# Second attention of a fused attention and MoE kernel: the exps' key blocks added by VectorE before the row sums

## The chip, the cores and the metric

The kernel runs on one core of one Trainium2 chip. The metric is the device time of one execution in microseconds (us), the median of three runs; lower is better.

## The reference

Attention with a soft cap, for q, k, v of shape (4 batches, 12 heads, 448, 64), is followed by two dense layers (each with a nonlinear part between two matrix products):

```python
scores = scale * np.matmul(q, k.transpose(0, 1, 3, 2))
scores = cap * np.tanh(scores / cap)
scores = scores - np.max(scores, axis=-1, keepdims=True)
attn = np.exp(scores)
attn = attn / (np.sum(attn, axis=-1, keepdims=True) + 1e-09)
return np.matmul(attn, v).astype(np.float32)
...
x = np.ascontiguousarray(attn_out.transpose(0, 2, 1, 3)).reshape(B * S, H * D)
x = _moe_ref(x=x, **moe_kwargs)
return _moe2_ref(x=x, **moe2_kwargs)
```

The sums of the exps over the keys (`np.sum(attn, ...)`) are what this case is about.

## The kernel before

The work is done in two halves of two batches each (`hb` 0 and 1, from line 657). A half is `attention`, then `moe1`, then `moe2`. The last block of the first half's `moe2` is woven into the start of the second half's attention (`rest`).

`attention` (line 229) goes over 12 pairs of heads, p = 0 to 11 (n = 12). The 448 keys of a head are three blocks of 128 and one of 64; the scores are kept with the keys on the partitions and the 448 queries on the columns. A pair has seven score tiles of 128x448: for each of the three full blocks one tile for each head (b = 2r + hh), and one tile x that holds the 64-key blocks of both heads (64 partitions for each). They lie in `t[:, 0..6]`, with `t[:, 6]` from x.

The functions of a pair, in the order of the data:
- `load`, `load_v`, `fetch`: DMAs from POOL's queue (q and k, v, and weights for the next stage). `kq` and `vf` have three buffers.
- `split_qk` (252): VectorE writes the high and low part of q and k (`kqh`, `kql`), two operations of 960 columns.
- `scores` (265): TensorE, 18 matmuls into six PSUM banks (`s`), then three for x into a bank of tag `o`.
- `tanh` (286), `exp` (296): ScalarE, x first and then the two halves of `s`; one exp over all seven tiles, in place in `t`.
- `values` (301): TensorE, 16 fp32 matmuls on four 32-column tiles; the trace records two matmuls for each fp32 matmul.
- `sums` (309): TensorE with columns of ones as weights. For each of the two heads the three full blocks and the shared one are summed: eight matmuls on four 32-column tiles in two accumulating rounds, so that partitions 0 and 64 hold the two partial sums of head 0 and 32 and 96 those of head 1. For the last pair the tiles have 64 columns, and all four blocks of a head accumulate into its 64 partitions (lines 312 to 318).
- `evict_v` (326): VectorE copies the values out of PSUM. `evict_s` (332): ScalarE copies the sums out of PSUM (97 partitions), and SP issues two DMAs that spread them over 56 partitions (`rs`).
- `finish1` (339): VectorE adds the two partial sums and takes the reciprocal; SP writes them to DRAM (`rd`). `finish2` (346): SP reads them back over all partitions (`rb`). `finish3` (357): VectorE multiplies the values, and writes the high and low part (`xh`, `xl`) for the next stage, three operations. The last pair takes `finish_last`.

The order of every engine's work inside `attention` is that of the program text (`manual_schedule`, line 660). The loop at line 383 runs i from -5 to 11; in one iteration each function works for another pair:

```python
at(i, values)
at(i + 1, tanh)
at(i, sums)
at(i - 2, finish1)
at(i - 3, finish2)
at(i - 5, finish3)
at(i + 3, split_qk)
at(i, evict_v)
at(i + 2, scores)
at(i + 1, exp)
...
at(i, evict_s, m=n - 1)
```

`at` leaves out pairs below 0 or from 12 on, so that `finish3` starts with i = 5 and `split_qk` ends with i = 8. PSUM has eight banks: six for `s` and two for tag `o`, which values, sums and x take in turn: x of pair i + 2 comes into the bank of the values of pair i, the values of pair i + 1 into that of the sums of pair i, and the sums of pair i + 1 into that of x of pair i + 2. After the loop come the `finish` functions that are left (lines 406 to 414). `moe1` (422) is not ordered by hand: its first matmuls (`first`, line 438; recorded at lines 434 and 436) are woven by the program's scheduler into the last iterations. They go over batch 0 of the half with three column blocks, then over batch 1 in steps, the pairs finished last at the end.

Of the kernel before, what the change touches and what calls it, by code (L numbers as in the profile page):

```python
# [9 lines left out]
F32 = mybir.dt.float32  # L10
# [4 lines left out]
ALU = mybir.AluOpType  # L15
# [14 lines left out]
def fused_kernel(ctx, tc, qk_in, v, cap, w1, w2, w3, w4, gln, out):  # L30
    nc = tc.nc
    B, H, S, D = 4, 12, 448, 64
    DM = H * D
    P = 128
    CP = 56
    Q = 32
# [22 lines left out]
    psum = {}  # L59
# [30 lines left out]
    ones = const.tile([P, 3, D], F32, name="ones")  # L90
# [50 lines left out]
    def early():  # L141

        units = [(f"1_{c}_{half}_{i}", w1u[(c * 2 + half) * (NK // 2) + i])
                 for c in range(2) for half in range(2) for i in range(NK // 2)]
        units += [(f"2_0_{d}", w2u[d]) for d in range(NK)]
        units = units[:WA]
        stage = {}

        def fetch(k):
            key, src = units[k]  # L150
            if key in saved:
                w = wp.tile([P, 2, 512], F32R, tag="w", name="w")
                nc.gpsimd.dma_start(w.bitcast(F32), saved[key].bitcast(F32))
                ahead[key] = w
            else:
                stage[k] = words(src, nc.sync if k == 0 else nc.gpsimd)

        def high(k):
            key = units[k][0]
            if k in stage:  # L160
                w = wp.tile([P, 2, 512], F32R, tag="w", name="w")
                ahead[key] = w
                stage["f", k] = narrowed(stage.pop(k))

        def mid(k):
            if ("f", k) in stage:
                nc.scalar.copy(ahead[units[k][0]][:, 0], stage["f", k])

        def low(k):
            if ("f", k) in stage:  # L170
                key = units[k][0]
                w = ahead[key]
                nc.vector.tensor_tensor(w[:, 1], stage.pop(("f", k)), w[:, 0].bitcast(F32), ALU.subtract)
                pending.append((key, w))

        return fetch, high, mid, low
# [52 lines left out]
    def attention(ap, hb, xh, xl, rest=None):  # L229
        pairs = [(bb, j) for bb in range(HB) for j in range(NP)]  # L230
        n = len(pairs)
        raw, qk, vs, sc, ts, os_, so, fin, rss, rds, rbs = ({} for _ in range(11))
        fetch, high, mid, low = early()

        def load(p):
# [73 lines left out]
        def sums(p):  # L309
# [9 lines left out]
            for rr in range(2):  # L319
                for g in range(4):  # L320
# [2 lines left out]
                    w = ones[:, 0, :Q] if r < 3 else ones[:, 1 + hh, :Q]  # L323
                    nc.tensor.matmul(o[cs, :S], w, t[:, 6 if r == 3 else 2 * r + hh], start=(rr == 0), stop=(rr == 1))  # L324

        def evict_v(p):
            if p < n - 1:
                ou = ap.tile([P, S], F32, tag="ou", name="ou", bufs=7)
                nc.vector.tensor_copy(ou, os_.pop(p)[:, :S])
                fin[p] = ou  # L330

        def evict_s(p):
            su = ap.tile([P, S], F32, tag="su", name="su", bufs=2)
            nc.scalar.copy(su[:3 * Q + 1], so.pop(p)[:3 * Q + 1, :S])
            rs = rss[p] = ap.tile([CP, 2, 2 * S // CP], F32, tag="rs", name="rs", bufs=4)
            for k in range(2):
                nc.sync.dma_start(rs[:, k], su[2 * Q * k:2 * Q * k + Q + 1:Q])
# [39 lines left out]
        def at(p, fn, *a, m=n):  # L377
            if 0 <= p < m:
                fn(p, *a)
# [3 lines left out]
        for i in range(-5, n):  # L383
            e = i + 2
            at(i, values)
            at(i + 1, tanh)
            at(i, sums)
            at(i - 2, finish1)
            at(i - 3, finish2)
            at(i - 5, finish3)  # L390
            at(i + 3, split_qk)
            at(i, evict_v)
            at(i + 2, scores)
            at(i + 1, exp)
            if hb == 0 and i == 0:
                nc.scalar.activation(gcol, guard, AF.Exp)
            if rest and i == -1:
                rest[2]()
            at(i, evict_s, m=n - 1)
            at(e - 2, mid, m=WA)  # L400
            at(i + 5, load)
            at(e, fetch, m=WA)
            at(i + 3, load_v)
            at(e - 3, low, m=WA)
            at(e - 1, high, m=WA)
# [251 lines left out]
    for hb in range(2):  # L657
        xh, xl = xtiles()
        with pools(f"a{hb}", ("t",), ("kqh", "kql"), ("ou",), ("rb", "rs", "su"), None) as ap, banks(f"pa{hb}", ("s", 2), ("o", 2)):
            with tc.manual_schedule(engines=ORD):  # L660
                attention(ap, hb, xh, xl, rest)
        yh, yl = xtiles()
        if hb == 0:
            nc.sync.dma_start(glt, gln.rearrange("(c p) -> p c", p=P))
        with pools(f"m{hb}", ("gh", "gl"), ("wx",), ("acc",), None) as mp, banks(f"pm{hb}", ("a", 2), ("b", 2)):
            moe1(mp, xh, xl, yh, yl)
        with pools(f"n{hb}", ("h2g",), ("wx",), ("lh0", "ll0"), None, ("e",), ("lh1", "ll1")) as mp, banks(f"pn{hb}", ("a", 2), ("b", 2)):
            rest = moe2(mp, hb, yh, yl)
# [63 lines left out]
```

## Time and profile before

| | |
|---|---|
| median of three runs | 913.27 us (913.23 to 913.3) |
| profiled execution | 918.84 us |
| its span | 917.1 us |
| mean granted clock of TensorE | 0.999 |
| TensorE busy | 911.1 us (99%) |
| VectorE busy | 584.3 us (64%) |
| ScalarE busy | 420.8 us (46%) |
| POOL busy | 46.7 us (5%) |

The span runs from the first to the last instruction of the profiled execution. Times in rows are us from the start of the span. PE is TensorE, ACT is ScalarE, DVE is VectorE. The second attention goes from about 452 to 554 us.

### The profile page before, as it was taken

Reading aid. Unit: us, or ns where it says so; the run is one execution under the profiler, and the core shown is the slowest. Engines: PE = TensorE matmul, PEld = TensorE weight load, DVE = VectorE, ACT = ScalarE, POOL = GpSimd, SP = SyncE. Lnnn points to the kernel's source line nnn. Section 1 sums busy time; section 2 is a strip of 40 time slices with the busy share of each in tenths; the row PEclk is TensorE's granted clock in tenths of the full one; section 3 lists DMA queues with packets and bytes.
Section 4 is the critical chain, followed back from the end, with each engine's and each line's share of the span. In section 5 each row is a group of like instructions: output and inputs, shape, how many; then the busy total and the mean of one; then the engine's idle time right before and its main releaser. Section 6 shows DMA issues by size and latency. Waiting matters only on the chain.

```text
span 917.1 us, 13131 instructions
## 1 busy us (share of the span) xinstructions
PE 911.1 (99%) x5258; PEld 732.8 (80%) x5258; DVE 584.3 (64%) x919; ACT 420.8 (46%) x480; POOL 46.7 (5%) x88
## 2 busy tenths in 40 slices
PE   8999999999999999999999999999999999999998
PEld 5444699999999988888854448999999999888887
DVE  6687989999999990987334535881452634306751
ACT  6999276555263322343278880862421502113311
POOL 2211000000000000001122100000000000000000
PEclk9999999999999999999999999999999999999999
DMA  8554680795875972730255532333232332231301
GB/s 286 182 179 149 235 309 24 240 366 175 294 256 194 304 242 101 245 132 36 108 208 193 176 90 89 126 120 111 92 115 92 126 105 93 69 115 42 130 36 51
DMA packets 46424, 142.98 MB, mean 156 GB/s; under 512 B 10460, under 2 KB 13532, under 8 KB 46364
## 3 DMA queue, kind: packets, MB, share of 16 engines
q1 hardware_dynamic: 39180, 112.95, 36.3%
q0 software_dynamic: 7040, 29.20, 9.2%
q8 instruction: 41, 0.67, 0.3%
q14 instruction: 19, 0.16, 0.1%
q10 hardware_dynamic: 144, 0.00, 0.0%
HBM read 98.64 MB, written 43.33 MB: 155 GB/s over the span
## 4 chain that ended last, share of the span: by engine, by line
PE 98%; DMA 1%; ACT 0%; DVE 0%; issue 0%
PE hp L434 17%; PE op L490 17%; PE hp L436 9%; PE op L492 9%; PE o L307 8%; PE s L275 5%; PE hp L227 4%; PE hp L225 4%; PE hp L226 4%; PE so L324 4%; PE oab L594 2%; PE oab L590 2%; PE oab L591 2%; PE x L281 2%; PE tp L539 1%; PE oab L592 1%
## 5 line engine op out<-in xcount | busy, mean ns | idle before, releaser
L434 PE MATMUL hp<-xl,w 128*128 128x448 f32 x384 | 116.3, 369 | 0.0
L434 PE MATMUL hp<-xh,w 128*128 128x448 f32 x384 | 116.2, 369 | 0.0
L436 PE MATMUL hp<-xh,w 128*128 128x448 f32 x384 | 115.9, 368 | 0.0
L492 PE MATMUL op<-gh,w 128*128 128x448 f32 x336 | 96.8, 368 | 0.0
L490 PE MATMUL op<-gh,w 128*128 128x448 f32 x336 | 96.6, 368 | 0.0
L490 PE MATMUL op<-gl,w 128*128 128x448 f32 x336 | 96.6, 368 | 0.0
L434 PEld LDWEIGHTS hp<-xh,w 128*128 128x128 f32 x384 | 72.1, 188 | 8.8 <-issue 1.5
L434 PEld LDWEIGHTS hp<-xl,w 128*128 128x128 f32 x384 | 72.1, 188 | 8.6 <-issue 1.4
L307 PE MATMUL o<-t,vf 128*32 128x448 f32 x768 | 77.8, 542 | 0.1
L436 PEld LDWEIGHTS hp<-xh,w 128*128 128x128 f32 x384 | 72.1, 188 | 7.2
L299 ACT ACTIVATE t<-t,shift,capt 128x3136 f32<-128x3136 f32 (+2 forms) x26 | 72.7, 2806 | 0.7
L499 DVE TENSOR_TENSOR acc<-op,acc 128x448 f32<-128x448 f32 x72 | 42.1, 622 | 46.9 <-PE op L492 46.7
L490 PEld LDWEIGHTS op<-gh,w 128*128 128x128 f32 x336 | 63.1, 188 | 6.4
L490 PEld LDWEIGHTS op<-gl,w 128*128 128x128 f32 x336 | 63.1, 188 | 6.4
L492 PEld LDWEIGHTS op<-gh,w 128*128 128x128 f32 x336 | 63.1, 188 | 6.3
L292 ACT ACTIVATE t<-s,tscale 128x1344 f32<-128x1344 f32 x48 | 63.5, 1378 | 6.3 <-PE s L275 6.3
L225 PE MATMUL hp<-w,xh 128*128 128x512 f32 x168 | 65.5, 390 | 0.0
L227 PE MATMUL hp<-w,xl 128*128 128x512 f32 x168 | 65.4, 389 | 0.0
L226 PE MATMUL hp<-w,xh 128*128 128x512 f32 x168 | 65.4, 389 | 0.0
L462 ACT ACTIVATE u<-hp 128x896 f32<-128x896 f32 x32 | 29.4, 920 | 75.8 <-PE hp L436 75.8
L468 DVE SCALAR_TENSOR_TENSOR gf<-u,hp 128x896 f32<-128x896 f32 x32 | 34.9, 1089 | 45.5 <-ACT t L464 45.5
L476 ACT CAST gh<-gf 128x896 fp32r<-128x896 f32 x32 | 30.2, 945 | 72.7 <-PE op L492 49.2
(150 smaller groups left out, 1645.8 us busy)
## 6 DMA issues: line engine op xcount, KB each, us to landing
d<-w SPq DMA_DIRECT2D x69, 512.0 KB
w<-d SPq DMA_DIRECT2D x56, 512.0 KB
st<-in_moe_w_out_dram SPq DMA_DIRECT2D x35, 512.0 KB
st<-in_moe_w_in_dram SPq DMA_DIRECT2D x25, 512.0 KB
kq<-in_qk_dram POOLq DMA_DIRECT2D x21, 480.0 KB, 4.2
w<-d POOLq DMA_DIRECT2D x13, 512.0 KB, 5.1
st<-in_moe_w_in_dram POOLq DMA_DIRECT2D x11, 512.0 KB, 5.2
vf<-in_v_dram POOLq DMA_DIRECT2D x22, 256.0 KB, 2.9
```

What stands on the lines that cost most here:

```text
L225: nc.tensor.matmul(ps, sh, mh, start=first, stop=False)
L226: nc.tensor.matmul(ps, sh, ml, start=False, stop=False)
L227: nc.tensor.matmul(ps, sl_, mh, start=False, stop=last)
L275: nc.tensor.matmul(s[b // 3][:, b % 3, :S], st[rows, cs], mv[rows, KW:], start=first, stop=last)
L292: nc.scalar.activation(t[:, 3 * half:3 * half + 3], s[half][:, :, :S], AF.Tanh, scale=tscale)
L299: nc.scalar.activation(t[:, sl], t[:, sl], AF.Exp, bias=shift, scale=capt)
L307: nc.tensor.matmul(o[cs, :S], vf[:, r, cs], t[:, 6 if r == 3 else 2 * r + g // 2], start=(r == 0), stop=(r == 3))
L434: nc.tensor.matmul(hp[:, g, :S], wh[:, ms], xs[g][i], start=(kk == 0 and i == 0), stop=False)
L436: nc.tensor.matmul(hp[:, g, :S], wl[:, ms], xs[g][0], start=False, stop=(kk == NK - 1))
L490: nc.tensor.matmul(op[:, g, :S], wh, gg[i][:, g], start=(m == 0 and i == 0), stop=False)
L492: nc.tensor.matmul(op[:, g, :S], wl, gg[0][:, g], start=False, stop=(m == nm - 1))
L499: nc.vector.tensor_tensor(a, op[:, g, :S], a, ALU.add)
```

## The change

It concerns the second attention alone (`hb` 1). A new function `presum` lets VectorE add the three full key blocks of each head, `t[:, 0:2]`, `t[:, 2:4]` and `t[:, 4:6]`, into a tile `m` of 128x896 (two adds, the second in place). `sums_added` takes the place of `sums`: the ones multiply `m` and the shared block, four matmuls in one round of four 32-column tiles for a pair, and for the last pair four matmuls on 64-column tiles. `presum` of pair i + 1 stands after its exp in the loop. `evict_s` copies by VectorE instead of ScalarE, and stands directly after `evict_v` instead of after the exp.

```diff
+        def presum(p):
+            t = ts[p]
+            m = sm[p] = ap.tile([P, 2, S], F32, tag="sm", name="sm", bufs=2)
+            nc.vector.tensor_tensor(m, t[:, 0:2], t[:, 2:4], ALU.add)
+            nc.vector.tensor_tensor(m, m, t[:, 4:6], ALU.add)
+
+        def sums_added(p):
+            t, m = ts.pop(p), sm.pop(p)
+            o = so[p] = psum["o"].tile([P, 512], F32, tag="o", name="so")
+            if p == n - 1:
+                for hh in range(2):
+                    nc.tensor.matmul(o[D * hh:D * (hh + 1), :S], ones[:, 0], m[:, hh], start=True, stop=False)
+                for hh in range(2):
+                    nc.tensor.matmul(o[D * hh:D * (hh + 1), :S], ones[:, 1 + hh], t[:, 6], start=False, stop=True)
+                return
+            for g in range(4):
+                hh = g % 2
+                w, b = (ones[:, 0, :Q], m[:, hh]) if g < 2 else (ones[:, 1 + hh, :Q], t[:, 6])
+                nc.tensor.matmul(o[Q * g:Q * (g + 1), :S], w, b, start=True, stop=True)
+
...
-            nc.scalar.copy(su[:3 * Q + 1], so.pop(p)[:3 * Q + 1, :S])
+            (nc.vector.tensor_copy if hb else nc.scalar.copy)(su[:3 * Q + 1], so.pop(p)[:3 * Q + 1, :S])
...
-            at(i, sums)
+            at(i, sums_added if hb else sums)
...
             at(i, evict_v)
+            if hb:
+                at(i, evict_s, m=n - 1)
             at(i + 2, scores)
             at(i + 1, exp)
+            if hb:
+                at(i + 1, presum)
...
-            at(i, evict_s, m=n - 1)
+            if not hb:
+                at(i, evict_s, m=n - 1)
```

## Rows read from the trace of the kernel before

**Rows 1.** The page: busy time by engine; the chain's shares by engine.
```profile
PE 911.1 (99%) x5258; PEld 732.8 (80%) x5258; DVE 584.3 (64%) x919; ACT 420.8 (46%) x480; POOL 46.7 (5%) x88
...
PE 98%; DMA 1%; ACT 0%; DVE 0%; issue 0%
```

**Rows 2.** The chain that ended last, one loop iteration: start, us, engine, tile, line.
```profile
474.29 3.15 PE o L307 x32
477.44 1.50 PE so L324 x16
478.94 2.02 PE s L275 x18
480.96 0.82 PE x L281 x3
481.78 3.14 PE o L307 x32
```

**Rows 3.** ScalarE's timeline, one iteration and the last exp: start, us [idle before, releaser].
```profile
504.28 0.64 ACT L290 ACTIVATE t<-x,tscale 128x448 f32<-128x448 f32 x1 [0.86 <-PE x L281]
...
507.49 3.01 ACT L299 ACTIVATE t<-t,shift,capt 128x3136 f32<-128x3136 f32 x1
510.40 0.51 ACT L334 COPY su<-so 97x448 f32<-97x448 f32 x1
...
544.92 3.01 ACT L299 ACTIVATE t<-t,shift,capt 128x3136 f32<-128x3136 f32 x1
```

**Rows 4.** VectorE's timeline over the same iteration.
```profile
504.28 0.66 DVE L257 CAST kqh<-kq 128x960 fp32r<-128x960 f32 x1 [1.71 <-PE x L281]
504.97 1.16 DVE L258 TENSOR_TENSOR kql<-kq,kqh 128x960 fp32r<-128x960 f32 x1
507.45 0.62 DVE L329 COPY ou<-o 128x448 f32<-128x448 f32 x1 [1.32 <-PE o L307]
508.00 0.22 DVE L341 SCALAR_TENSOR_TENSOR rs<-rs,gcol 56x16 f32<-56x16 f32 x1
508.25 0.24 DVE L342 RECIPROCAL rs<-rs 56x16 f32<-56x16 f32 x1
508.42 0.55 DVE L366 TENSOR_TENSOR ou<-ou,rb 128x448 f32<-128x448 f32 x1
509.00 0.39 DVE L367 CAST xh<-ou 128x448 fp32r<-128x448 f32 x1
509.43 0.63 DVE L368 TENSOR_TENSOR xl<-ou,xh 128x448 fp32r<-128x448 f32 x1
```

**Rows 5.** The chain at the loop's end: seven hp matmuls, last values, last sums.
```profile
546.32 0.60 PE hp L434 x2
...
547.74 0.20 PE hp L434
547.98 3.21 PE o L307 x32
551.19 3.16 PE so L317 x16
```

**Rows 6.** VectorE on 896 columns: timeline in the MoE stage; groups of the whole run.
```profile
577.17 1.09 DVE L472 SCALAR_TENSOR_TENSOR gf<-w,gf 128x896 f32<-128x896 f32 x1
578.18 1.08 DVE L471 TENSOR_TENSOR t<-hp,t 128x896 f32<-128x896 f32 x1
579.30 1.23 DVE L473 COPY_PREDICATED gf<-mk,t 128x896 f32<-128x896 uint8 x1
...
L477 DVE TENSOR_TENSOR gl<-gf,gh 128x896 fp32r<-128x896 f32 x32 | 34.8, 1091 | 26.8 <-ACT gh L476 25.9
```

**Rows 7.** Wait instructions before the values, whole run: ns min/median/max.
```profile
L307 PEldq EVENT_SEMAPHORE  x24: 51/51/1277, 11.2 to 544.3; - x24
```

**Rows 8.** After the loop: VectorE's last finish3; ScalarE's first activation of the next stage.
```profile
563.01 0.63 DVE L368 TENSOR_TENSOR xl<-ou,xh 128x448 fp32r<-128x448 f32 x1
...
574.21 0.92 ACT L462 ACTIVATE u<-hp 128x896 f32<-128x896 f32 x1 [25.87 <-PE hp L436]
```

More of the change, by code (lines that the diff above doesn't have):

```diff
@@ L231, in attention @@
         n = len(pairs)
-        raw, qk, vs, sc, ts, os_, so, fin, rss, rds, rbs = ({} for _ in range(11))
+        raw, qk, vs, sc, ts, os_, so, fin, rss, rds, rbs, sm = ({} for _ in range(12))
         fetch, high, mid, low = early()
```

## The prediction

> **What bounds the kernel now.** I read the page first, then the chain that ended last over the second attention, then the timelines of ScalarE and VectorE for one iteration of its loop, last the end of the loop. The page says that TensorE is busy for 99% of the span and holds 98% of the chain [rows 1], so time comes off only where TensorE gets less to do, or is lost where it starts to wait. The chain through one iteration is TensorE without a hole: values 3.15 us, sums 1.50, the next scores 2.02, their shared block x 0.82 [rows 2], together 7.49 us, and the next values begin 7.49 us later. The reader should see that no other engine is in it.
>
> ScalarE starts a pair's tanh when its x is done (504.28) and ends the exp at 510.50, that is 6.22 us later; then comes the copy of the sums (0.51 us), and 0.86 us were waited for x [rows 3]. VectorE works in two pieces and waited 1.71 us before the first [rows 4]. Neither is far from TensorE's period: that is what decides this case.
>
> At the end of the loop the exp of pair 11 runs to 544.92 + 3.01 = 547.93 [rows 3], and values(11) begin at 547.98 [rows 5]: they wait for ScalarE, with 0.05 us from the recorded end to the start. The gap before them, from 546.32, is filled by seven matmuls of the next stage [rows 5].
>
> **Sums on TensorE.** A pair's sums are 8 fp32 matmuls on 32-column tiles, recorded as 16, in 1.50 us [rows 2]: four steps of four tiles, 0.375 each. The change leaves 4 matmuls, recorded as 8, two such steps: 0.75 us. Eleven pairs give 11 x 0.75 = 8.25 us. The last pair works on 64-column tiles, 16 records in 3.16 us [rows 5]; 8 stay, so 1.58 us goes. Gross 9.83 us, and TensorE's iteration becomes 6.74 us. No gain beyond this is to be had, since nothing else leaves TensorE. The same number of switches between tile shapes stays, so I price them at nothing.
>
> **ScalarE** loses 11 copies of 0.51 us. It gains nothing in time: tanh starts with x. But its 6.22 + 0.05 us from x to the values must now fit in 6.74, which leaves 0.47. It fits.
>
> **VectorE** gains the copy of the sums and two adds of 128x896 for each pair. What counts is the distance from start to start. From the timeline [rows 4]: split 0.69 + 1.08, copy of the values 0.55, the two small steps of finish1 0.25 + 0.17, the three of finish3 0.58 + 0.43 + 0.55, together 4.30 us. Where an idle time follows, I took the recorded time less 0.08, as in the MoE stage, where an operation of 1.09 us is followed after 1.01 by one that doesn't need it and one of 1.08 after 1.12 by one that does [rows 6]. The copy of the sums has the width of the copy of the values and also reads PSUM: 0.55. The adds have no row of their own. The nearest is the subtraction with two fp32 operands in SBUF over the same 896 columns, 1.091 us [rows 6]; the second add needs the first, so 1.12 + 1.01 = 2.13 for the pair. From below: the in-place product over 448 columns took 0.55, and from 448 to 960 columns a subtraction grew from 0.63 to 1.16, 1.04 ns per column [rows 4], so an add is 1.01 and the pair about 1.96. From above: the copy with a mask over 896 columns, 1.23 [rows 6], so about 2.40. I take 2.13, since that row has the same operand places and size.
>
> VectorE's iteration is then 4.30 + 0.55 + 2.13 = 6.98 us against TensorE's 6.74. But this full load occurs in few iterations: finish3(i-5) exists from i = 5, split_qk(i+3) up to i = 8. Outside i = 5 to 8 VectorE has at most 5.4 us and the cover is there. In these four the copy of the values comes late for x(i+2), which takes over its PSUM bank (two banks hold values, sums, x in turn), and TensorE waits 0.24 us each: 0.96 us. With the bounds of the adds it is 0.3 to 2.0 us.
>
> Rows show that VectorE's next operation starts 0.08 us before the recorded end of the one before it, where it doesn't need its result [rows 6]. The Trainium skill ("VectorE: DVE Perf Modes", The DRAIN you can't avoid) speaks against this: the next operation does not start until the pipe is empty, though it allows that one which is not held starts earlier. By that rule in its strict form the load would be the sum of the recorded durations, 7.27 us, the wait 4 x 0.53 = 2.1 us and the time 905.6 us. The trace has the overlap, so the sum above stays.
>
> **The waits that are moved.** The adds stand in VectorE's queue behind both copies and wait for the exp; queued behind them are finish1, finish3, the split and the next copy of the values. The exp ends 6.27 us after its x, which with a period of 6.74 is 0.47 before the next values start; the adds end 1.66 after it, and the sums need them at 3.15. So TensorE does not wait for the adds. The copy of the sums now frees a bank from VectorE instead of ScalarE: the next values wait for it, but in a full iteration it ends 0.55 after the copy of the values, while x alone takes 0.82. The sums' two DMAs on SP keep their place among SP's other DMAs and are issued earlier. POOL's loads wait as before on the values and on the split, iterations ahead of their use. Values wait now on two engines (exp, copy of the sums); should each cost one more wait instruction, 51 ns [rows 7], that is 0 to 0.6 us. I take 0: the values have such a wait now, one for each pair, and the chain goes from x to values without a hole (480.96 + 0.82 = 481.78).
>
> **The end.** sums(10) become 0.75 us shorter, but values(11) follow exp(11), whose start is tied to x(11). The gap grows by 0.75 us. The seven matmuls fit the old gap within 0.05 us, so I take it that the order, made outside the hand-written part, follows the gap's length and puts three or four more there; else 0.75 us is lost. VectorE's tail begins one pair of adds later. It ended at 563.64, while the first activation of the next stage waited until 574.21 [rows 8]. Ahead of that lie 12 matmuls at 0.20 us [rows 5] which need the pair that VectorE finishes last, so they start some 8 us after the tail; 2.1 us of adds and 1.6 us from TensorE coming earlier fit under that.
>
> **Sum.** 8.25 + 1.58 - 0.96 = 8.87 us. The profiled execution took 918.84 us (span 917.1), 5.57 more than the median 913.27; the stage worked on is the same, so I take the difference off the median: 904.4 us.
>
> **Rivals.**
> *VectorE binds harder.* For it: 0.24 us of excess rests on overlaps of hundredths, and each late x also delays tanh, exp and the next adds. A full circle (x 0.82, tanh and exp 6.27, adds 2.13, finish 1.98, split 1.77, copy 0.62 and 0.05 of signal) is 13.6 us for two periods, 6.82 each, so little has to be added to it. Against: five of the eleven iterations have no finish3 and two no split. If these four keep the old 7.49, the loss is 3.0 us; with waits of 0.6 for values and the end's 0.75 the gain is 5.5, 907.8 us; with adds at their upper bound alone it is 7.8, 905.5 us. The Trainium skill ("TensorEngine Tiling (Array Packing)", PSUM Bottleneck) says that after tiling the copy out of PSUM may become the bottleneck and that both ScalarE and VectorE are to be used for it; here both copies go to VectorE. Of itself that is the 0.55 us counted above: the trace bears it out only in so far as VectorE's load passes TensorE's.
>
> *The gap at the end is not filled.* 905.1 us. Against it stands the good fit of the seven.
>
> *Slower: the adds cost double.* Two fp32 streams out of SBUF beside ScalarE's long in-place exp could go at half rate. Pair 4.26: a full iteration 9.11, so 2.37 x 4; in the others the circle without finish3 is (9.99 + 4.26) / 2 = 7.13, 0.39 over, x 6. Loss 11.8 against 9.83: 915.3 us. It decides from about 1.9 us for an add; the 1.091 of [rows 6], a mean over 32, is against it.
>
> *Hardly a gain.* The step of four tiles costs 0.375 us in a stream of four; if two in a row keep a fixed part, or adds lie between 1.5 and 1.9 us, the change does not bring what its count says: about 912.
>
> **How the numbers follow.** Forecast 0.50, own range 903.4 to 905.4; gap unfilled 0.17; VectorE harder 0.25; hardly a gain 0.04; slower 0.04. The gross gain of 9.83 sets the lower end, 903.3 with a tenth for the spread of the runs; VectorE's case sets the upper, 907.8; outside are the last two cases and a tail. Within 0.2%, about what a measurement of this kernel can tell, is 911.4 to 915.1. So faster 0.92, same 0.04, slower 0.04.
>
> **What would show it.** Sums in the chain at 0.75 us for 8 records and 1.58 for the last; a period of 6.74 up to i = 4, near 7.0 in i = 5 to 8, then 6.74; in these four a wait of x on the copy of the values, and nowhere on the adds; adds of 1.0 to 1.1 us; ten or eleven matmuls before values(11). Wrong would be: adds over 1.2 us, values waiting on the exp or the copy of the sums in every iteration, a period over 7.0 in the light ones, or the next stage waiting for VectorE's tail.

## The result and the profile after

| | before | after |
|---|---|---|
| median, us (runs) | 913.28 (6; 911.55 to 915.42) | 904.91 (6; 903.03 to 908.23) |
| ratio, 95% interval | | 0.9904 (0.9886 to 0.9923) |
| profiled execution, us (span) | 918.84 (917.1) | 907.26 (905.5) |
| first scores of the second attention | 452.51 | 450.31 |
| ScalarE's first activation behind it | 574.21 | 563.13 |
| the stage between them | 121.70 | 112.82 |

The median fell by 8.37 us, where 8.87 was forecast. The two profiled executions differ by 11.58, and only 8.88 of that lies in the stage that was changed: the second attention began 2.20 us earlier, and 0.50 came behind the stage. A total spreads over some microseconds from run to run; the stage moved by 0.2 to 0.3 (a second trace of the changed kernel, below, has 112.51, one of the kernel before 121.47). The stage is therefore the measure in what follows, taken in every trace from the same two instructions.

The page of the changed kernel, busy time by engine and the chain's shares, against [rows 1]:

```profile
PE 897.6 (99%) x5162; PEld 727.9 (80%) x5162; DVE 613.4 (68%) x954; ACT 416.7 (46%) x469; POOL 48.1 (5%) x88
...
PE 84%; DVE 10%; DMA 3%; issue 1%; ACT 1%; SPq 0%; DVEq 0%
```

TensorE lost 13.5 us of busy time and VectorE gained 29.1; the matmul records fell by 96, that is 11 x 8 + 8. VectorE's 10% of the chain are only in small part this change: 18 us of them lie in the second attention, some 73 in the first half, which is the same in both kernels. The chain's shares differ between executions of one kernel: the second trace of the kernel before (last experiment) has TensorE at 88% and VectorE at 8%, where [rows 1] has 98% and 0%.

The chain of the changed kernel through one early iteration, against [rows 2]:

```profile
471.36 3.15 PE o L307 x32
474.51 0.75 PE so L344 x8
475.26 2.05 PE s L275 x18
477.31 0.81 PE x L281 x3
478.12 3.14 PE o L307 x32
```

The sums take 0.75 us where they took 1.50, and the next values begin after 6.76 us instead of 7.49. Nothing but TensorE is in it. One of the full iterations looks different. The timeline of VectorE, changed kernel, against [rows 4] (L349 copies the values, L354 the sums, L329 and L330 are the adds):

```profile
503.80 0.62 DVE L349 COPY ou<-o 128x448 f32<-128x448 f32 x1
504.33 0.61 DVE L354 COPY su<-so 97x448 f32<-97x448 f32 x1
504.86 1.08 DVE L329 TENSOR_TENSOR sm<-t 128x896 f32<-128x896 f32 x1
505.98 1.09 DVE L330 TENSOR_TENSOR sm<-sm,t 128x896 f32<-128x896 f32 x1
506.99 0.22 DVE L361 SCALAR_TENSOR_TENSOR rs<-rs,gcol 56x16 f32<-56x16 f32 x1
507.24 0.24 DVE L362 RECIPROCAL rs<-rs 56x16 f32<-56x16 f32 x1
507.41 0.55 DVE L386 TENSOR_TENSOR ou<-ou,rb 128x448 f32<-128x448 f32 x1
508.00 0.39 DVE L387 CAST xh<-ou 128x448 fp32r<-128x448 f32 x1
508.43 0.63 DVE L388 TENSOR_TENSOR xl<-ou,xh 128x448 fp32r<-128x448 f32 x1
508.97 0.66 DVE L257 CAST kqh<-kq 128x960 fp32r<-128x960 f32 x1
509.66 1.16 DVE L258 TENSOR_TENSOR kql<-kq,kqh 128x960 fp32r<-128x960 f32 x1
510.73 0.62 DVE L349 COPY ou<-o 128x448 f32<-128x448 f32 x1
```

No idle time is noted on any of these lines: VectorE runs without a hole, and its round, from copy to copy, is 6.93 us. That is longer than TensorE's 6.74 to 6.76, so TensorE waits. The round before it, the first that holds both finish3 and the split, still had a hole:

```profile
497.91 1.09 DVE L329 TENSOR_TENSOR sm<-t 128x896 f32<-128x896 f32 x1 [1.35 <-ACT t L299]
```

There VectorE waited 1.35 us for the exp, and from then on had no idle time until the copy at 503.80. In this first iteration it is the path from the exp over the adds, finish and split to the copy that is late for x, in the next three VectorE's load. The view of the waits over the second attention, changed kernel (who waited, for whom: us in total, times, longest; PEld is TensorE loading the weights of a matmul, and `issue` stands where no engine was waited for):

```profile
DVE sm L329 <- ACT t L299: 12.4, 8, 2.0
...
PEld x L281 <- issue: 2.2, 7, 0.3
PEld x L281 <- DVE ou L349: 2.0, 4, 0.5
```

x waits four times for the copy of the values, 0.5 us each; in the other seven iterations the same step idles 0.3 us for no engine. The excess is 0.2 us, four times. The adds themselves wait for the exp eight times and let nobody wait. The distances from values to values, all ten up to the last pair, show where the four are (worked out from the starts of L307 in the timeline):

```
before   7.49 7.48 7.49 7.49 7.48 7.49 7.48 7.49 7.49 7.48
after    6.75 6.76 6.75 6.75 6.76 6.97 6.93 6.94 6.94 6.75
```

The chain at the end of the loop, changed kernel, against [rows 5] (the first and last of the hp matmuls ahead of the last values):

```profile
536.81 0.60 PE hp L459 x2
...
538.86 0.41 PE hp L459 x2
539.27 3.17 PE o L307 x32
542.44 0.90 PE so L337 x4
543.34 0.75 PE so L339 x4
```

Eleven hp matmuls fill the gap, where seven did. The last sums take 1.65 us, where they took 3.16.

### The profile page after: what moved, and what is told of

Read it like the earlier page. It is cut to its first block, busy times and chain, and to the rows that moved or that the text cites. A ratio compares the mean times of both kernels' runs of the same rounds, so it can differ in the third digit from the quotient of the medians.

```text
span 905.5 us, 12979 instructions
## 1 busy us (share of the span) xinstructions
PE 897.6 (99%) x5162; PEld 727.9 (80%) x5162; DVE 613.4 (68%) x954; ACT 416.7 (46%) x469; POOL 48.1 (5%) x88
## 4 chain that ended last, share of the span: by engine, by line
PE 84%; DVE 10%; DMA 3%; issue 1%; ACT 1%; SPq 0%; DVEq 0%
PE op L515 14%; PE hp L459 14%; PE op L517 7%; PE hp L461 7%; PE o L307 7%; PE hp L226 4%; PE hp L227 4%; PE hp L225 4%; PE s L275 4%; PE oab L615 2%; PE oab L619 2%; PE oab L616 2%; PE so L324 2%; DMA st<-in_moe_w_out_dram 2%; PE x L281 2%; PE tp L564 1%
## 5 line engine op out<-in xcount | busy, mean ns | idle before, releaser
L307 PE MATMUL o<-t,vf 128*32 128x448 f32 x768 | 77.8, 542 | 0.0
```

The source lines that it names most:

```text
L307: nc.tensor.matmul(o[cs, :S], vf[:, r, cs], t[:, 6 if r == 3 else 2 * r + g // 2], start=(r == 0), stop=(r == 3))
```

## The experiments

The changed kernel has, with its own line numbers, `sums_added` at 332, the copies at 349 and 354, the order of the loop from 404. The edits are against it.

**Adds alone.** TensorE makes the old sums, VectorE does all the new work:

```diff
-            at(i, sums_added if hb else sums)
+            at(i, sums)
```

> TensorE keeps the old sums (8 matmuls a pair), VectorE makes the adds (their result is not read) and copies the sums. The measure is the stage: from the first scores of the second attention to ScalarE's first activation of the next stage; before 121.70 us, after 112.82 us. Theory (the gain is TensorE's time alone; VectorE's 6.94 us in a full iteration hides under 7.49): period 7.49 throughout, no wait of x on VectorE's copy, stage 121.5 to 122.0 us. Rival (the adds cost time by themselves, through VectorE's queue or by slowing ScalarE's exp, and the gain has to be larger than the count to come out as it did): stage above 122.5 us. A second rival (it was the copy of the sums leaving ScalarE that shortened the period): stage clearly below 121 us.

Measured: stage 121.39 us, all ten periods 7.48 or 7.49. The chain of this run, and VectorE's next adds in its timeline:

```profile
505.28 3.14 PE o L307 x32
508.43 1.50 PE so L324 x16
509.93 2.02 PE s L275 x18
```

```profile
511.57 1.09 DVE L329 TENSOR_TENSOR sm<-t 128x896 f32<-128x896 f32 x1 [0.46 <-ACT t L299]
```

With 7.49 us to hide under, VectorE's work costs nothing: it waits 0.46 us for the exp even in a full iteration. Under this cover, neither the adds nor the copy's move to VectorE changes the time. 121.39 is 0.1 under the range named, but a second trace of the kernel before has 121.47 (last experiment), so it is the same.

**No adds.** The opposite:

```diff
-            t, m = ts.pop(p), sm.pop(p)
+            t = ts.pop(p)
+            m = t[:, 0:2]
...
-            if hb:
-                at(i + 1, presum)
```

> The two adds are left out: the sums take the first key block and the shared one only, so the second and third key blocks are missing from the row sums. Everything else as in the changed kernel. Theory (in the iterations i = 5 to 8 VectorE's load of 6.94 us sets the period, 6.74 elsewhere): all periods 6.74 to 6.77, no wait of x on the copy of the values, stage 0.7 to 1.0 us shorter than after's 112.82, so 111.8 to 112.1. Rival (the longer periods of i = 5 to 8 come from something else, such as the bank handed over by VectorE's copy of the sums or the DMAs of finish2): they stay near 6.94, stage 112.6 to 113.

Measured: stage 112.04 us, periods 6.72 to 6.75 in all ten. The waits of this run:

```profile
PEld x L281 <- issue: 2.2, 7, 0.3
PEld x L281 <- DVE ou L387: 1.2, 4, 0.3
```

The four waits on VectorE (here put down to L387, an operation of finish3) are there by name, but last 0.3 us like the idle time of the other seven: the excess is gone. The long periods of the full iterations came from the adds in VectorE's queue. That the stage lies in the range named shows less, since two other differences offset each other in it: 0.55 us were lost ahead of the first values (14.78 us from the first scores, where the changed kernel has 14.23), where TensorE waited for VectorE's L636 in the matmuls of the first half that are woven in, and 0.36 us less passed behind the last values (23.55 against 23.91), in the pace told at the end. The periods are what this run shows.

**The adds twice.** Two more adds for each pair, ahead of the real ones:

```diff
+            nc.vector.tensor_tensor(m, t[:, 0:2], t[:, 2:4], ALU.add)
+            nc.vector.tensor_tensor(m, m, t[:, 4:6], ALU.add)
             nc.vector.tensor_tensor(m, t[:, 0:2], t[:, 2:4], ALU.add)
             nc.vector.tensor_tensor(m, m, t[:, 4:6], ALU.add)
```

> Each pair's two adds are made twice (the first time for nothing): VectorE's load grows by 2.2 us a pair. Theory (VectorE's load is the bound wherever it passes TensorE's 6.74): the full load becomes 9.1 us for i = 5 to 8, 7.0 to 7.6 for the others (5.4 + 2.2 with finish1), so 4 x 2.15 + 3 x 0.85 + 2 x 0.4 + 2 x 0.6 = 13 us more than after, stage 125 to 127 us, slower than before. Rival (from the prediction: only the full iterations are paid, the others give room up to a circle of 7.13): 8.6 + 6 x 0.39 = 11 us, stage 123 to 124.5. Rival (the adds lie in VectorE's idle time before the exp and a second pair costs little): stage below 118.

Measured: stage 127.85 us, above all the ranges and nearest to the theory's; the one execution took 919.17 us. Two rounds of VectorE in this run's timeline without finish3:

```profile
486.72 1.08 DVE L329 TENSOR_TENSOR sm<-t 128x896 f32<-128x896 f32 x1
...
494.28 1.08 DVE L329 TENSOR_TENSOR sm<-t 128x896 f32<-128x896 f32 x1
```

A light round is 7.56 us, the last three full periods 9.18 to 9.19 (the first 8.82): near what the theory has (7.6 and 9.1). What it missed is 2.0 us at the end: the distances before the last two pairs were 7.92 and 7.01, where the changed kernel has 6.75 and 6.38 and the expectation had 0.6 more for each, and from the last values to the next activation it took 25.28 instead of 23.91 us, with waits of the next stage's matmuls for an xh of VectorE's tail (1.0 to 1.4 us in the waits). It also shows that the prediction's slower rival was priced too low. It let the light iterations give room up to 7.13; VectorE's own load of 7.56 is the larger bound. The point at which the gain is gone lies below two pairs of adds, as it said, but on other grounds.

**The copy of the sums on ScalarE, after the exp:**

```diff
-            (nc.vector.tensor_copy if hb else nc.scalar.copy)(su[:3 * Q + 1], so.pop(p)[:3 * Q + 1, :S])
+            nc.scalar.copy(su[:3 * Q + 1], so.pop(p)[:3 * Q + 1, :S])
...
-            if hb:
-                at(i, evict_s, m=n - 1)
...
-            if not hb:
-                at(i, evict_s, m=n - 1)
+            at(i, evict_s, m=n - 1)
```

> The copy of the sums goes back to ScalarE, after the exp, with the adds as in the changed kernel. VectorE's full load falls to 6.4 us, below TensorE's 6.74. ScalarE's copy ends 6.67 us after its pair's x in the trace of before, and the next values, which need its PSUM bank, can start 0.05 later, at 6.72. Theory (the engines are sums of their distances, and 6.72 still fits into 6.74): period 6.74 to 6.80 throughout, stage 111.8 to 112.4 us, 0.4 to 1.0 us faster than after. Rival (ScalarE has no room for it: the tanh that follows waits for the copy, and every iteration gets longer): period 7.0 or more in all ten iterations, stage 114.5 us or more. This also tests the rule that both engines are to share the copies out of PSUM.

Measured: stage 112.14 us; median 904.95 us, ratio to before 0.9884 (0.9834 to 0.9934). The stage is within the theory's range, but the periods are not all: 6.79, 6.76, 6.77, 6.74, 6.77, then 6.93, 6.79, 6.91, 6.79, then 6.77. The waits of this run:

```profile
PEld o L307 <- ACT su L354: 3.3, 10, 0.4
...
PEld x L281 <- DVE ou L349: 1.6, 4, 0.5
```

ScalarE's copy now ends last before the values, by a few hundredths: 6.72 did fit, as worked out. But x still waits for VectorE, in every other full iteration, though VectorE's load is below 6.74. The four average 6.86 us. The chain of this run goes around there:

```profile
495.80 3.02 ACT t L299
498.84 1.10 DVE sm L329
...
504.81 0.55 DVE ou L349
505.39 0.89 PE x L281 x3
506.31 0.64 ACT t L290
...
509.52 3.02 ACT t L299
```

From exp to exp these are 13.72 us for two pairs. That is the circle over two periods which the prediction had among its rivals at 6.82: x, tanh and exp, adds, finish, split, copy, x. VectorE's load sets 6.94 with the copy of the sums, the circle 6.86 without it. Of the 0.37 to 0.68 us by which this stage is shorter than the changed kernel's, only 0.2 to 0.3 lie ahead of the last values (88.60 us from the first scores, against 88.79 and 88.91); the rest lies behind them, in the pace told at the end.

**The same copy ahead of the exp,** where the change has it in the text, but on ScalarE (only the first two lines of the edit above).

> The copy of the sums stands where the change put it in the text (before the exp), but on ScalarE. Theory (a wait in a queue costs what is queued behind it): the copy waits for the sums, which end 3.90 us after the values began, so the exp behind it starts at about 4.4 instead of 3.25, ends at 7.41, and the next values begin at 7.46: period 7.4 to 7.5 in all ten iterations, stage 118 to 120 us, most of the gain lost although TensorE does as little as in the changed kernel. Rival (ScalarE's waits are covered as long as its work of 6.7 us is below TensorE's 6.74, wherever the copy stands): period below 6.95, stage below 114 us.

Measured: stage 120.9 us, all ten periods 7.52 or 7.53. ScalarE's timeline of this run:

```profile
504.30 2.65 ACT L292 ACTIVATE t<-s,tscale 128x1344 f32<-128x1344 f32 x2
507.97 0.53 ACT L354 COPY su<-so 97x448 f32<-97x448 f32 x1 [1.02 <-PE so L344]
508.40 3.01 ACT L299 ACTIVATE t<-t,shift,capt 128x3136 f32<-128x3136 f32 x1
511.31 0.62 ACT L290 ACTIVATE t<-x,tscale 128x448 f32<-128x448 f32 x1
```

The copy waits 1.02 us for the sums and the exp stands behind it, and the values wait for the exp. TensorE does as little as in the changed kernel, and almost the whole gain is gone: one place in one queue is worth as much as the change itself. The stage came out 0.9 above the range; the period was 0.06 longer than worked out, and the last distance, before pair 11, 7.74.

**Finish behind the copy.** With the copy on ScalarE after the exp, finish1, finish2 and finish3 of the second attention go behind `evict_v`. To the circle's 13.6 us they then add nothing. The first run of it also had the first attention's last pair with adds (told next); the second run not.

```diff
-            at(i - 2, finish1)
-            at(i - 3, finish2)
-            at(i - 5, finish3)
+            if not hb:
+                at(i - 2, finish1)
+                at(i - 3, finish2)
+                at(i - 5, finish3)
             at(i + 3, split_qk)
             at(i, evict_v)
             if hb:
-                at(i, evict_s, m=n - 1)
+                at(i - 2, finish1)
+                at(i - 3, finish2)
+                at(i - 5, finish3)
```

> Copy of the sums on ScalarE after the exp, finish1 and finish3 of the second attention behind the copy of the values in VectorE's order, and the first attention's last pair as in the run beside it. Theory (the periods of 6.91 to 6.93 us which stayed with the copy on ScalarE come from the circle over two periods exp, adds, finish, split, copy of the values, x; with the 1.98 us of finish out of it the circle is 5.8 a period): all periods 6.74 to 6.80, no wait of x on VectorE, stage 111.4 to 112.0 us, and 1.5 us less in the first half; in all 2.3 to 3.0 us below the changed kernel. Rival (the 6.9 come from ScalarE, whose work and waits fill its period to the last tenth): periods stay at 6.8 to 6.93, stage 112.1 or more.

> The copy of the sums on ScalarE after the exp and the two finish steps behind the copy of the values, in the second attention; the first attention as it was. Theory: stage as in the run with both changes, 111.6 to 112.0 us, against 112.5 and 112.8 for the changed kernel, and nothing lost in the first half (25.8 to 26.3 us there); in all 0.5 to 1.0 below the changed kernel, which its total can hardly show over a spread of some us. Rival (the reorder gives the time back behind the loop, where VectorE's tail comes later): stage 112.5 or more.

Measured: stage 111.88 and 111.86 us, all periods 6.73 to 6.79 in both. The waits of the second run, and ScalarE's timeline there:

```profile
PEld o L307 <- ACT su L354: 3.4, 10, 0.4
PEld x L281 <- issue: 2.8, 9, 0.3
```

```profile
501.93 3.01 ACT L299 ACTIVATE t<-t,shift,capt 128x3136 f32<-128x3136 f32 x1
504.84 0.51 ACT L354 COPY su<-so 97x448 f32<-97x448 f32 x1
505.49 0.63 ACT L290 ACTIVATE t<-x,tscale 128x448 f32<-128x448 f32 x1
```

No x waits for VectorE any more. What is left over 6.74 is put down to ScalarE by the waits, and ScalarE now has no idle time noted in its round. In the stage this version is 0.65 us better than the best trace of the changed kernel, 0.48 of it up to the last values (88.31 against 88.79 us). In the total it can't be shown: the second run has a median of 905.13 us (ratio 0.9913, 0.988 to 0.9945), the first 907.44 (0.9927, 0.9901 to 0.9954). The first run's forecast for the total, 2.3 to 3.0 us below the changed kernel, failed: the 1.5 us of the first half did not come (26.38 us from its last values to the next activation, against 25.86 and 26.23).

**The first attention's last pair.** There the adds would have room, it seemed, and 1.5 us of TensorE's time would go:

```diff
-            at(i, sums_added if hb else sums)
+            at(i, sums_added if hb or i == n - 1 else sums)
...
             at(e - 1, high, m=WA)
+            if not hb and i + 1 == n - 1:
+                presum(n - 1)
```

> The changed kernel, and in the first attention the last pair alone gets the adds and the shorter sums; VectorE makes these adds after its other work of that iteration. Measure: from the start of the first attention's last values to ScalarE's first activation behind it, 26.23 us before and 25.86 after. Theory (8 of the 16 records on 64-column tiles go, 1.58 us, and VectorE has room at that place): 1.4 to 1.7 us less, 24.2 to 24.6. Rival (VectorE is late there, because the weights it prepares for the next stage are due, or the adds hold the sums up): 25.5 us or more. The second attention's stage stays at 112.5 to 113.

Measured: 26.18 us from the first attention's last values to the next activation, so the rival's case; the second attention's stage 112.36 us, a little under the range named. The waits behind the first attention in this run:

```profile
PEld hp L461 <- DVE xh L387: 1.7, 1, 1.7
...
PE hp L461 <- DVE xh L387: 1.3, 1, 1.3
```

VectorE's tail there is without a hole, and two adds in it push pair 9's xh past the time when TensorE wants it. A last try, on the version with the finish behind the copy, put that pair's finish3 ahead of the 2.95 us reciprocal:

```diff
-        finish_last(n - 1)
+        if hb:
+            finish_last(n - 1)
         finish3(n - 3)
+        if not hb:
+            finish_last(n - 1)
```

> The same, and the first attention's last pair with adds again, now with pair 9's finish3 ahead of the long reciprocal of the last pair in VectorE's tail. Theory (the attempt before failed because the first half's next stage waited 1.7 us for pair 9's xh, which the adds had pushed back): that wait goes, and the stretch from the last values to the next activation is 24.2 to 24.9 us, against 25.86 and 26.23. Rival (another pair or the weights that VectorE prepares are then the late ones): 25.3 us or more.

The wait for xh is gone, but the stretch is 26.64 us, by its number again the rival's case. It doesn't compare, though: the scheduler wove the next stage's matmuls in another order, and 109 of them are recorded between the last values and the activation, where the other traces have 96 or 97. At 0.203 us each, the 12 or 13 more are 2.4 to 2.6 us, so this run neither shows the theory nor refutes it. The second attention began at 454.50 us, later than in any trace with the first half as it was (449.63 to 454.12), and the median is 910.01 us (0.9944, 0.9914 to 0.9974), beside 905.13 for the version without it on the same chip. The intervals of the two overlap; no gain is to be seen.

**Both kernels again.**

> The changed kernel unaltered, beside the runs above on the same chip. The stage is ordered by waits between engines and not by chance, so 112.7 to 113.0 us again; the total follows whatever the parts outside the stage do on this chip, 903 to 908 us.

> The kernel before, unaltered, for a second trace. In its first trace a matmul of 448 columns behind the loop came every 0.207 us, in most traces of the other kernels every 0.203. If this belongs to an execution and not to the kernel, it can be 0.203 here, and then the stage is 121.3 to 121.5 us instead of 121.70, and the stretch behind the first attention's last values 25.86 instead of 26.23; if it belongs to the kernel, 121.70 and 26.23 again.

Measured: the changed kernel has a stage of 112.51 us and periods of 6.72 to 6.75 and 6.93 to 6.99, a median of 905.32 us, ratio 0.9908 (0.9888 to 0.9928). The kernel before has 121.47 us, and 26.23 again behind the first attention. By these second traces the change is worth 8.96 us in the stage, by the first 8.88.

## Why the prediction was right

- **Sums on TensorE.** 0.75 us each, eleven times, as counted; the last pair 1.65 instead of 1.58. Gross 9.76 instead of 9.83.
- **Adds.** Start to start 1.12 and 1.01, the pair 2.13 us, to the hundredth what the row of the MoE stage gave; the copy of the sums 0.53 for 0.55. The full round of VectorE is 6.93 to 6.94 instead of 6.98.
- **Where it binds.** In i = 5 to 8 and nowhere else. The four distances exceed 6.74 by 0.82 us together, forecast 0.96. Leaving the adds out takes this away, so it is not the hand-over of the bank. In the last three, VectorE's round without a hole shows its load, as counted. In the first it was the path from the exp; the prediction's sum had no term for that, and that its 0.23 us came near the 0.24 counted is luck.
- **The adds' own wait** costs nobody anything: no wait of the sums on them is listed for the changed kernel. It took twice the adds to make TensorE wait there, up to 1.0 us a time.
- **The gap at the end.** The order followed the gap: eleven matmuls for seven, and 6.38 us between the last two values before and after. The rival of the unfilled gap did not occur.
- **The strict rule of the pipe** ("VectorE: DVE Perf Modes", The DRAIN you can't avoid, in the Trainium skill) would have given a full round of 7.27 us. Measured is 6.93: VectorE's operations which don't need the one before them start 0.07 to 0.09 us before its recorded end here too. The sentence of that page which lets an operation that isn't held start earlier fits this, the strict one doesn't.
- **VectorE binds harder** was wrong in its size, 0.2 us and not 0.75 a period. Its circle is real, though: it stayed hidden under VectorE's load of 6.94 and came out as 6.86 when the load was taken down. The page "TensorEngine Tiling (Array Packing)" of the Trainium skill, section PSUM Bottleneck, wants both engines for the copies. Here giving one back to ScalarE was worth 0.2 to 0.3 us up to the last values, and 8.1 to 8.4 us of the stage were lost where the copy stood in front of the exp: in these runs the advice paid only with the right place in the queue.

The sum by the measured terms: 8.25 + 1.51 - 0.82 = 8.94 us for the stage, measured 8.88 and 8.96. Two misses, 0.07 less gain at the last pair and 0.14 less loss in the full iterations, partly offset each other in that. The total's 8.37 differs from it by less than its spread; that the median came within 0.5 us of the forecast is in part luck, since six runs of the changed kernel spread over 5.2 us.

## What to carry to other kernels

Before work is moved from the bounding engine to a free one, write down the free engine's round from start to start, iteration by iteration: it may be full in only some of them, and here the price was about the difference of the two rounds there and nothing elsewhere. Then follow the circle through all engines, since it becomes the bound as soon as the load is taken off. A moved copy must not stand in front of what the next step waits for: the same 0.5 us copy on ScalarE cost nothing that shows or some 8 us, by its place in one queue.

## What had not been expected

The totals spread on both sides of the stage. Ahead of it, the second attention's first scores came between 449.63 and 454.12 us in ten traces of kernels whose first half is the same. In the MoE stages there VectorE prepares weights, and it is nearly full, in the table by stretches of the kernel before (us; busy time and count of PE, PEld, DVE, ACT, POOL; clock, DMA share, GB/s):

```profile
100.00:200.00 100.00, 100.00 (x485) 89.71 (x482) 93.14 (x131) 53.68 (x73) 0.00 (x0) 1.00 0.67 236
200.00:300.00 100.00, 100.00 (x485) 90.83 (x485) 96.24 (x145) 43.57 (x58) 0.00 (x0) 1.00 0.71 243
```

With VectorE at 93 to 96% while TensorE is recorded as busy throughout in this trace, two adds more in front of it may well cost what TensorE saves. No run tests this by itself, and none shows what moves the first scores by 4.5 us.

Behind the first attention the matmuls of 448 columns came every 0.207 us in both traces of the kernel before and in that of the copy ahead of the exp, and every 0.203 us in the changed kernel's two traces and most others, at a granted clock of 1.00 in that stretch either way. Over the stretch of 26 us that is 0.37 us. Behind the second attention the kernel before had both (26.23 and 25.86 us from its last values), so it does not belong to the kernel alone.

The same two paces make up the spread behind the stage. From ScalarE's first activation there to the end of the span nine traces take 338.1 to 338.2 us, and four 342.0 to 342.9: the first trace of the kernel before, both of the changed kernel, and the run with adds in the first attention's last pair. The kernel before in its first and its second trace, in the same columns as above:

```profile
600.00:700.00 100.00, 100.00 (x486) 90.83 (x485) 44.29 (x47) 35.35 (x46) 0.00 (x0) 1.00 0.33 107
600.00:700.00 100.00, 100.00 (x495) 92.69 (x494) 46.72 (x49) 36.91 (x47) 0.00 (x0) 1.00 0.32 109
```

TensorE is busy throughout at the same granted clock, yet makes 2% fewer matmuls in the first. So up to 4.7 us of a total, half of what this change is worth, come and go with the pace behind the stage, and some tenths inside it: the changed kernel took 23.91 and 23.72 us behind its last values, with the run of the first attention's last pair at 23.54. What decides the pace is open.
